# One statistic of LayerNorm moved behind a cast in VectorE's queue, in the first microseconds of an attention kernel

## The chip, the cores and the metric

The kernel runs on one core of one Trainium2 chip. The metric is the device time of one execution in microseconds (us), lower is better. Executions of one kernel are compared only in the undisturbed ("fast") state; all runs told here were in it, with a granted TensorE clock of 0.998 to 1.0. The "span" in a profile is the part of the execution that the profiler covers; in all runs here it is about 1.8 us shorter than the time.

Names: PE is TensorE's matmul side, PEld its weight loads, DVE is VectorE, ACT is ScalarE, POOL is GpSimd, SP is SyncE, whose queue issues many of the DMAs. "Landing" is the moment at which a DMA's data has arrived.

## The reference, cut to what matters

```python
xn = layernorm(A_x)                          # x: 2048 x 640
q  = (xn @ wq) -> 32 heads of 192
o  = softmax(q @ k_cache.T * 192**-0.5) @ v_cache   # per head, 2048 queries, 2048 keys
g  = silu( (silu(xn @ w1) * (xn @ w3)) @ w2 )
out = A_x + (o @ wo) * g
```

All is bfloat16. Attention over 32 heads is nearly the whole work.

## The kernel before

The kernel works through 32 heads, in each through four blocks `qb` of 512 queries, in each block through eight pairs `p` of key tiles. x is normalised in four blocks of 512 rows, `g` = 0 to 3, each of four tiles of rows. Block 0 and half of block 1 are normalised before the loop, the rest during head 0, between its matmuls. So during head 0 VectorE has two jobs: the LayerNorm of the next blocks, and the casts that take projected queries out of PSUM.

PSUM tiles with the tag `st2` share two buffers. Scores, projections and the transposes of x all take one of them in turn, so a late release of one of these tiles stops PE.

```python
def ln_stats(g, i):                      # VectorE: mean and variance of tile i of block g
    ...
    xr = x_sb[:, 4 * g + i, :].rearrange("p (a f) -> p a f", a=nsub)
    for a in range(nsub):
        nc.vector.bn_stats(out=stats[:, a, :], in_=xr[:, a, :])
    nc.vector.bn_aggr(out=mv[:, i, :], in_=stats[:])
    ...

def ln_turn(g, i2, copy):                # PE turns two normalised tiles; `copy` takes them from PSUM
    pst = ps_st.tile([P, 2, DC, P], BF16, tag="st2", name="pst")
    ...  # 10 transposes
    copy(out=xnT[...], in_=pst[:])

def swap_halves(g):                      # xnS is xnT with its partition halves exchanged, by DMA
    nc.sync.dma_start(out=xnS[0:64, :, qs], in_=xnT[64:P, :, qs])
    nc.sync.dma_start(out=xnS[64:P, :, qs], in_=xnT[0:64, :, qs])

def two_products(W, qs):                 # projection of a later head, in two row groups of 64
    ps = ps_st.tile([P, 1024], F32, tag="st2", name="ps")
    for j in range(2 * DC):
        for r in range(2):
            rows = slice(r * 64, (r + 1) * 64)
            xs = xnT if j % 2 == r else xnS
            nc.tensor.matmul(ps[:, r * 512:(r + 1) * 512], lhsT=W[rows, j, :], rhs=xs[rows, j // 2, qs],
                             start=(j == 0), stop=(j == 2 * DC - 1))
    return ps

def cast_pair(qAB, ps):                  # the two halves of ps, on two engines
    a = nc.vector.tensor_copy(out=qAB[0][:], in_=ps[:, 0:512])
    b = nc.scalar.copy(out=qAB[1][:], in_=ps[:, 512:1024])
    ...

# head_start(), before the loop; the order on SyncE's queue matters here
    ...
    swap_halves(0)
    ...
    load_v(0, (1,))        # second half of head 0's V, 384 KB, wanted at pair 4
    load_x(2)              # rows of block 2, 640 KB
    ...
    ln_turn_dma(1, 0); ln_turn_dma(1, 1)     # two tiles of block 1 turned by DMA
    for g in range(3, NQB):
        load_x(g)

def first_head(qb, p):                   # called at the end of each pair of head 0
    if qb == 0 and p == 1:
        ln_norm(1, 2, nc.vector)
        ln_norm(1, 3, nc.vector)
    if qb == 0 and p == 3:
        ln_turn(1, 1, nc.vector.tensor_copy)
        swap_halves(1)
    g = qb + 2
    if g < NQB:
        i = p - 2 if qb == 0 else p - 1
        if 0 <= i < 4:
            ln_stats(g, i)
        ...

for n, (h, qb, p) in enumerate(stream):
    ...
    if h == 0 and qb == 0 and p == 3:
        project(1, 0)                    # two_products, cast_pair, then moves of the result
    if h == 0 and qb + 1 < NQB and p == (5 if qb == 0 else 4):
        project0(qb + 1)                 # head 0's next queries, from xnT alone
    scores(n + 2)
    values(n)
    ...
    if h == 0:
        first_head(qb, p)
```

## Time and profile before

| | before |
|---|---|
| median of the first three runs | 1939.9 us (1939.57 to 1941.53) |
| the execution that was profiled | 1939.16 us, span 1937.4 us |
| PE busy in the span | 1927.5 us |
| PE's wait for the cast of head 1's first query | 0.75 us, once |

The page's first part gives busy time by engine, and its chain part says what the chain of work that ended last consists of:

```profile
span 1937.4 us, 59668 instructions
PE 1927.5 (99%) x27273; PEld 1316.9 (68%) x27281; DVE 654.4 (34%) x997; ACT 1180.1 (61%) x1278; POOL 282.4 (15%) x501
...
PE 98%; DMA 1%; DVE 1%; ACT 0%; SPq 0%; issue 0%; DVEq 0%; ACTq 0%
```

The chain is PE nearly throughout. Busy matmul time says little about how near PE is to its best, since pipelined matmuls look smaller in the trace (the Trainium skill, "Perfetto Trace Analysis", "Identifying the Most-Contended Engine", says so and asks for other measures; a_behind below has a loss of 0.42 us inside a stretch that counts as busy throughout). But the trace does show where PE stands still, and that is what this change is after. The list of PE's waits in the first 100 us (columns: who, on which line, for whom, total us, times, longest):

```profile
PE pk L569 <- POOL ident_bf masks.py:199: 2.8, 1, 2.8
PE pst L354 <- DVE qA L429: 0.8, 1, 0.8
PE st L487 <- ACT pT L490: 0.3, 1, 0.3
PE pst L354 <- DVE xn L346: 0.3, 1, 0.3
PE st L483 <- DVE qA L393: 0.2, 1, 0.2
```

The second line is the one. The timeline shows how it comes about. Its columns are start, duration, engine, line, operation, output and inputs, count; in brackets stands how long the engine was idle before and what ended that.

```profile
21.27 0.38 PE L424 MATMUL ps<-xnT,W 64*128 64x512 bf16 x1
...
21.69 0.58 ACT L430 CAST qB<-ps 128x512 bf16<-128x512 f32 x1 [1.74 <-PE ps L424]
...
21.97 0.89 DVE L316 BATCH_NORM_STATS2 stats<-x_all 128x6 f32<-128x320 bf16 x2 [0.60 <-DMA x_all<-in_A_x_dram]
22.12 0.84 PE L516 MATMUL obank<-vt,pT 64*128 64x193 bf16 x16
...
22.89 0.21 DVE L317 BATCH_NORM_AGGREGATE mv<-stats 128x2 f32<-128x12 f32 x1
23.02 0.64 DVE L429 CAST qA<-ps 128x512 bf16<-128x512 f32 x1
...
23.71 0.73 PE L354 MATMUL pst<-ident_bf,xn 128*128 128x128 bf16 x10 [0.75 <-DVE qA L429]
...
24.48 0.82 DVE L356 COPY xnT<-pst 128x1280 bf16<-128x1280 bf16 x1 [0.83 <-PE pst L354]
```

The projection (L424) is done at about 21.65 us. ScalarE casts its half at once. VectorE's cast is equally ready, but the statistics of block 2's first tile are ahead of it in VectorE's queue, and they wait until 21.97 us for the rows of block 2. PE ends its value products (L516) at 22.96 us and then needs the buffer for the transposes (L354), which can start only when the cast has ended, at 23.71 us.

### The profile page before, as it was taken

How to read it: one execution, taken by the hardware profiler on the slowest of the kernel's cores; microseconds unless marked ns; L12 is line 12 of the kernel's file. 1: busy time of each engine (PE TensorE's matmuls, PEld its weight loads, DVE VectorE, ACT ScalarE, POOL GpSimd, SP SyncE). 2: the span in 40 equal slices, each digit the busy share in tenths (PEclk: the TensorE clock that was granted, in tenths of full speed). 3: DMA queues.
4: the chain of work that ended last, by engine and by line, in shares of the span. 5: the costliest groups of instructions: out<-in, count | busy, mean ns of one | idle time of the engine just before them, and what ended most of it. 6: DMA issues, size and time to landing. Idle time of an engine off the chain costs nothing.

```text
span 1937.4 us, 59668 instructions
## 1 busy us (share of the span) xinstructions
PE 1927.5 (99%) x27273; PEld 1316.9 (68%) x27281; DVE 654.4 (34%) x997; ACT 1180.1 (61%) x1278; POOL 282.4 (15%) x501
## 2 busy tenths in 40 slices
PE   9999999999999999999999999999999999999998
PEld 6666666666666666666666666666666666577776
DVE  7333333333333333333333333333333334521111
ACT  6667676767676767776777777677767677210000
POOL 3111111111111111111111111111111110000000
PEclk9999999999999999999999999999999999999999
DMA  8643433323333434363434343434334220937872
GB/s 179 131 101 66 100 68 80 88 60 89 59 88 64 98 64 98 68 162 68 101 64 101 69 101 69 101 64 100 69 67 97 59 68 2 251 76 138 152 151 62
DMA packets 394643, 178.98 MB, mean 92 GB/s; under 512 B 341616, under 2 KB 382832, under 8 KB 394384
## 3 DMA queue, kind: packets, MB, share of 16 engines
q1 hardware_dynamic: 371136, 125.32, 31.5%
q0 software_dynamic: 19472, 45.71, 10.1%
q8 instruction: 215, 3.52, 0.8%
q10 hardware_dynamic: 3776, 4.06, 0.7%
q14 instruction: 44, 0.36, 0.1%
HBM read 52.82 MB, written 27.79 MB: 42 GB/s over the span
## 4 chain that ended last, share of the span: by engine, by line
PE 98%; DMA 1%; DVE 1%; ACT 0%; SPq 0%; issue 0%; DVEq 0%; ACTq 0%
PE obank L516 35%; PE st L487 33%; PE ps L424 14%; PE ps_s L111 11%; PE ps_f L727 3%; PE ps_gu L701 1%; DMA x_all<-in_A_x_dram 1%; PE st L488 1%; PE ps L410 0%; DVE stats L316 0%; ACT KW L277 0%; PE pst L354 0%; ACT xnT L356 0%; DVE qA L429 0%; SPq L289 0%
## 5 line engine op out<-in xcount | busy, mean ns | idle before, releaser
L490 ACT ACTIVATE pT<-st 128x1024 bf16<-128x1024 f32 x1024 | 1046.2, 1022 | 250.9 <-PE st L488 235.3
L516 PEld LDWEIGHTS <-pT 64*128 64x128 bf16 x16384 | 711.6, 94 | 241.9 <-ACT pT L490 0.2
L516 PE MATMUL obank<-vt,pT 64*128 64x193 bf16 x16384 | 849.6, 243 | 0.0
L487 PE MATMUL st<-qC,KW 64*128 64x512 bf16 x2046 | 605.8, 376 | 0.1
L525 DVE COPY osum<-obank 128x772 f32<-128x772 f32 x128 | 123.1, 962 | 787.1 <-PE obank L516 787.1
L488 PE MATMUL st<-qB,KW 64*128 64x512 bf16 x1024 | 385.2, 376 | 0.0
L487 PE MATMUL st<-qA,KW 64*128 64x512 bf16 x1022 | 384.5, 376 | 0.4 <-ACT pT L490 0.3
L488 PE MATMUL st<-qC,KW 64*128 64x512 bf16 x1022 | 384.5, 376 | 0.0
L488 PE MATMUL st<-qA,KW 64*128 64x512 bf16 x1022 | 384.4, 376 | 0.0
L487 PEld LDWEIGHTS <-KW 64*128 64x128 bf16 x3068 | 278.5, 94 | 153.7 <-issue 2.1
L424 PE MATMUL ps<-xnT,W 64*128 64x512 bf16 x1280 | 297.2, 376 | 0.0
L424 PE MATMUL ps<-xnS,W 64*128 64x512 bf16 x1280 | 296.3, 376 | 0.0
L488 PEld LDWEIGHTS <-KW 64*128 64x128 bf16 x3068 | 278.8, 94 | 0.7 <-issue 0.6
L377 POOL DMA_DIRECT2D qC<-qA x124 | 65.4, 527 | 1284.5 <-DVE rl_all L532 1268.3
L430 ACT CAST qB<-ps 128x512 bf16<-128x512 f32 x131 | 76.7, 585 | 228.2 <-PE ps L424 222.7
L111 PE MATMUL ps_s<-wo_sb,oT 128*128 128x384 bf16 (+3 forms) x1535 | 208.8, 299 | 0.1
L424 PEld LDWEIGHTS <-W 64*128 64x128 bf16 x2560 | 123.1, 94 | 121.1
L111 PEld LDWEIGHTS <-oT 128*128 128x128 bf16 x1536 | 148.3, 98 | 60.5
L526 DVE TENSOR_TENSOR osum<-osum,obank 128x772 f32<-128x772 f32 x128 | 122.7, 959 | 13.4
L533 DVE TENSOR_TENSOR ostage<-osum,rl_all 128x768 bf16<-128x768 f32 x128 | 122.6, 958 | 6.2 <-DMA o_scr<-ostage 1.9
L465 DVE SCALAR_TENSOR_TENSOR hT<-pt,qB 64x512 bf16<-64x512 bf16 x64 | 43.8, 684 | 197.4 <-ACT pt L464 197.4
L429 DVE CAST qA<-ps 128x512 bf16<-128x512 f32 x131 | 90.6, 691 | 25.0 <-PE ps L410 7.2
(84 smaller groups left out, 623.7 us busy)
## 6 DMA issues: line engine op xcount, KB each, us to landing
o_scr<-ostage SPq DMA_DIRECT2D x16, 1536.0 KB, 10.6
vt<-in_A_v_cache_dram SPq DMA_DIRECT2D x63, 384.0 KB, 6.0
qC<-qA POOLq DMA_DIRECT2D x248, 64.0 KB, 1.9
qC<-qB POOLq DMA_DIRECT2D x124, 64.0 KB, 2.4
wo_sb<-in_A_wo_dram POOLq DMA_DIRECT2D x1, 7680.0 KB, 37.3
W<-in_A_wq_dram POOLq DMA_DIRECT2D x32, 160.0 KB, 3.6
W<-in_B_w_dram POOLq DMA_DIRECT2D x32, 80.0 KB, 3.3
W<-in_A_wq_dram POOLq DMA_DIRECT2D x32, 80.0 KB, 2.9
```

The source lines that it names most:

```text
L111: nc.tensor.matmul(ps[:, 0:w], lhsT=oT[:, k, :], rhs=wo_sb[:, k, c0:c1], start=(k == 0), stop=(k == OC - 1))
L377: nc.gpsimd.dma_start(out=qC[0:64, half, :], in_=qAB[half][64:P, :])
L424: nc.tensor.matmul(ps[:, r * 512:(r + 1) * 512], lhsT=W[rows, j, :], rhs=xs[rows, j // 2, qs], start=(j == 0), stop=(j == 2 * DC - 1))
L429: a = nc.vector.tensor_copy(out=qAB[0][:], in_=ps[:, 0:512])
L430: b = nc.scalar.copy(out=qAB[1][:], in_=ps[:, 512:1024])
L487: nc.tensor.matmul(st2[:, 0:512], lhsT=ka, rhs=qa, start=r == 0 and nr == 3, stop=r == nr - 1)
L488: nc.tensor.matmul(st2[:, 512:1024], lhsT=kb, rhs=qb2, start=r == 0 and nr == 3, stop=r == nr - 1)
L490: nc.scalar.activation(out=pT2[:], in_=st2[:], func=ACT.Exp, scale=att_scale)
L516: nc.tensor.matmul(obanks[r][:, j * 256:j * 256 + DH + 1], lhsT=pT2[r * 64:(r + 1) * 64, t * 512 + j * P:t * 512 + (j + 1) * P], rhs=vt[r ...
L525: nc.vector.tensor_copy(out=osum[:], in_=ov[0])
L526: nc.vector.tensor_tensor(out=osum[:], in0=osum[:], in1=ov[1], op=ALU.add)
L533: nc.vector.tensor_tensor(out=ostage[:, qb * 4:qb * 4 + 4, hg * DH:(hg + 1) * DH], in0=osum[:, :, 0:DH], in1=rl.unsqueeze(2).to_broadcast( ...
```

## The change

The intent is to let the cast pass. The statistics of tile 0 of block 2 are no longer issued at the end of pair 2. They are issued at the end of pair 3, which is after the cast of the projection and before the copy of the transposes.

```diff
         if qb == 0 and p == 3:
+            ln_stats(2, 0)
             ln_turn(1, 1, nc.vector.tensor_copy)
             swap_halves(1)
         g = qb + 2
         if g < NQB:
             i = p - 2 if qb == 0 else p - 1
-            if 0 <= i < 4:
+            if 0 <= i < 4 and (qb, p) != (0, 2):
                 ln_stats(g, i)
```

No instruction is added or removed. On VectorE one cast goes ahead of two BN_STATS and one aggregation; no other engine's order changes.

## The prediction

> **What bounds the kernel now.** TensorE. The page gives PE 1927.5 us busy of a span of 1937.4, and the chain that ended last is 98% PE. From 80 us to the end of the attention (1750 us) PE is busy 1669.84 of 1670.00. So the only time to be had is in the few idle gaps of PE at the start. Quarter-microsecond stretches of the first 130 us show 4.67 us of PE idle: 2.77 before the first matmul, and after that only one large gap, 22.96 to 23.71 us. In the list of PE's waits it is "pst L354 <- DVE qA L429", 0.75 us (0.8 in the list), once.
>
> **How that gap comes about (timeline, 20 to 26 us).** In pair 3 of head 0's first block PE projects head 1's first query (L424, finished about 21.65). Its two halves lie in one PSUM buffer of two. ScalarE casts its half at once (21.69 to 22.27). VectorE's cast (0.64 us) stands in its queue behind the statistics of block 2's first rows, and these wait for the load of block 2's rows of x: VectorE idles 0.60 us until 21.97, then 0.89 us statistics, 0.21 aggregation. The cast runs 23.02 to 23.66. PE has ended the value products at 22.96, but its next transposes (L354) want the same PSUM buffer, so they start at 23.71. The Trainium skill, "PSUM — Partial Sum Buffer", section "Engine vs sequencer instructions", says that VectorE's queue is strict FIFO: a ready cast can't pass a waiting statistic. The trace agrees (cast ready at 21.69, started 23.02).
>
> **What the change does.** Nothing is added or removed. The order listing shows one difference on VectorE: the cast goes ahead of two BN_STATS and one aggregation. Other engines keep their order.
>
> Expected times, from those durations:
> - cast 21.7 to 22.35, before PE needs the buffer (22.96): the 0.75 us gap closes.
> - statistics from 22.35 (data landed 21.97) to about 23.45 with aggregation. The copy of the transposes (L356) gets its input 0.77 us after they start, about 23.72, so the statistics fit in front of it, with about 0.25 us to spare.
> - next scores need exp 5's PSUM buffer, whose exp ends at 23.41 as before; PE wants it at 23.63. Free.
> - copy 23.72 to 24.54, projection L410 about 25.05 instead of 25.80: the slack of 0.5 us stays.
> - query shifts (POOL) are issued 1.3 us earlier; no one waits for them.
>
> **How much stays.** Everything after hangs on PE, so all shifts by 0.75 us. Possible give-back: project(1,1) at 32.02 needs the swapped halves (second copy issued 26.01, 5.2 us to landing, so about 31.3); moved earlier they overlap more with the load of block 3 (issued 20.9, 5.4 us). Also L410 at 39.90 follows the DMA transposes' landing (39.75) by 0.15 us. Either may give back some tenths. I count 0.7 us.
>
> **Prediction.** 1939.9 - 0.7 = 1939.2 us, range 1938.3 to 1940.3. The spread of before (1939.57 to 1941.53) is larger than the gain, so the verdict is "same". Faster by over 2%: 0.005; within 2%: 0.99; slower: 0.005.
>
> **What the profile would show.** PE's wait "pst <- qA" gone (under 0.1 us), VectorE's 0.60 us wait for x_all gone or under 0.1, cast starting at about 21.7, transposes at about 22.96, L410 at about 25.05, PE idle after 20 us about 0.3 us instead of 1.05; total PE busy unchanged.
>
> **What would make it wrong.** x's block 2 landing over 1 us later, so that the copy of the transposes, not the cast, holds PE; a new wait at L424 (32 us) or L410 (40 us) for DMAs that do not come earlier; or run-to-run spread of a microsecond, which would hide the gain or reverse its sign.

## The result, and the profile after

| | before | after |
|---|---|---|
| median, six runs each | 1939.86 us | 1938.49 us |
| range | 1939.19 to 1941.53 | 1938.43 to 1939.14 |
| span of the profiled execution | 1937.4 us | 1936.7 us |
| PE idle from 20 to 130 us, in quarter-microsecond stretches | 1.04 us | 0.16 us |

(The 0.16 us are three gaps of 0.05 us, each in a group of ten L410 products of which the trace shows nine. So they may be missing records and not idle time; before has three such gaps too.)

The ratio of after to before is 0.9992 with a 95% interval of 0.9979 to 1.0005. A ratio is the mean time of one kernel's fast runs over that of the other's of the same rounds, so it is not quite the ratio of the medians in the table.

The page and the list of PE's waits of the changed kernel:

```profile
span 1936.7 us, 59668 instructions
PE 1927.1 (100%) x27273; PEld 1317.2 (68%) x27281; DVE 654.4 (34%) x997; ACT 1181.5 (61%) x1278; POOL 282.1 (15%) x501
...
PE 99%; DVE 0%; DMA 0%; ACT 0%; issue 0%
```

```profile
PE pk L569 <- POOL ident_bf masks.py:199: 2.8, 1, 2.8
PE pst L354 <- DVE xn L346: 0.8, 1, 0.8
PE st L487 <- ACT pT L490: 0.3, 1, 0.3
PE st L483 <- DVE qA L393: 0.2, 1, 0.2
```

The wait for `qA` at L429 is gone. (The wait for `xn` lies at 7 to 8 us, before the two kernels differ. The warm-up matmuls before it leave PE idle for longer or shorter; the transposes start at 7.8 and 7.9 us all the same.) The timeline, as before:

```profile
21.77 0.59 ACT L430 CAST qB<-ps 128x512 bf16<-128x512 f32 x1 [1.74 <-PE ps L424]
21.77 0.69 DVE L429 CAST qA<-ps 128x512 bf16<-128x512 f32 x1 [0.31 <-PE ps L424]
...
22.20 0.85 PE L516 MATMUL obank<-vt,pT 64*128 64x193 bf16 x16
22.38 0.88 DVE L316 BATCH_NORM_STATS2 stats<-x_all 128x6 f32<-128x320 bf16 x2
...
22.98 0.73 PE L354 MATMUL pst<-ident_bf,xn 128*128 128x128 bf16 x10
23.29 0.21 DVE L317 BATCH_NORM_AGGREGATE mv<-stats 128x2 f32<-128x12 f32 x1
...
23.75 0.82 DVE L356 COPY xnT<-pst 128x1280 bf16<-128x1280 bf16 x1 [0.25 <-PE pst L354]
```

Both casts start together at 21.77 us. The transposes follow the value products without a gap. VectorE still idles 0.25 us before the copy, so the statistics fit between the two. The transposes come 0.73 us earlier than before (22.98 against 23.71), and the span is 0.7 us shorter: nothing of it was given back in this execution.

The medians, however, differ by 1.37 us, twice the gap that the profile shows, and the changed kernel's runs lie closer together: five of six within 0.18 us. That was not predicted, and the experiments are about it.

### The profile page after: what moved, and what is told of

It reads as the page before. It is cut to its first block, busy times and chain, and to the rows that moved or that the text cites. A ratio compares the mean times of both kernels' runs of the same rounds, so it can differ in the third digit from the quotient of the medians.

```text
span 1936.7 us, 59668 instructions
## 1 busy us (share of the span) xinstructions
PE 1927.1 (100%) x27273; PEld 1317.2 (68%) x27281; DVE 654.4 (34%) x997; ACT 1181.5 (61%) x1278; POOL 282.1 (15%) x501
## 4 chain that ended last, share of the span: by engine, by line
PE 99%; DVE 0%; DMA 0%; ACT 0%; issue 0%
PE obank L516 35%; PE st L487 34%; PE ps L424 14%; PE ps_s L111 11%; PE ps_f L728 3%; PE ps_gu L702 1%; PE st L488 1%; PE ps L410 0%; DMA x_all<-in_A_x_dram 0%; DVE stats L316 0%; PE ps L391 0%; PE pst L354 0%; PE pk L271 0%; ACT pT L490 0%; DVE mv L317 0%
## 5 line engine op out<-in xcount | busy, mean ns | idle before, releaser
L488 PE MATMUL st<-qB,KW 64*128 64x512 bf16 x1024 | 385.0, 376 | 0.0
L488 PE MATMUL st<-qC,KW 64*128 64x512 bf16 x1022 | 384.3, 376 | 0.0
L488 PE MATMUL st<-qA,KW 64*128 64x512 bf16 x1022 | 384.3, 376 | 0.0
L424 PE MATMUL ps<-xnT,W 64*128 64x512 bf16 x1280 | 297.3, 376 | 0.0
L424 PE MATMUL ps<-xnS,W 64*128 64x512 bf16 x1280 | 296.2, 376 | 0.0
L488 PEld LDWEIGHTS <-KW 64*128 64x128 bf16 x3068 | 278.5, 94 | 0.8 <-issue 0.6
L424 PEld LDWEIGHTS <-W 64*128 64x128 bf16 x2560 | 123.6, 94 | 120.7
L429 DVE CAST qA<-ps 128x512 bf16<-128x512 f32 x131 | 90.6, 692 | 25.3 <-PE ps L410 7.2
```

The costliest lines, as they stand in the source:

```text
L488: nc.tensor.matmul(st2[:, 512:1024], lhsT=kb, rhs=qb2, start=r == 0 and nr == 3, stop=r == nr - 1)
```

## The experiments

Four calls, each on another chip, each with runs of the kernel before beside it. Every run below is "same" as the kernel before (each 95% interval of the ratio contains 1), so what follows rests on medians, spreads and traces. Names that start with `b_` are made from the kernel before, with `a_` from the changed one. The expectations name these theories.

- Theory L: PE's wait is for the load. The kernel before pays, microsecond for microsecond, for the landing of block 2's rows, which varies from run to run. The changed kernel has slack there.
- Rival N: the spread is noise that both kernels share, and the true gain is 0.75 us.
- Rival Q: not the load, but the place in the queue costs the time.
- Theory S and rival T came later: the slow runs that the changed kernel still has come from the swapped halves of block 0 landing late (S), or from elsewhere (T).

### The changed kernel again: a_again and a_third

No edit.

> The changed kernel once more, unchanged. Theory L (the kernel before pays, microsecond for microsecond, for when block 2's rows of x land, and that moment varies from run to run; the changed kernel has slack there): the changed kernel's runs lie within about 0.3 us of each other near 1938.5, those of the kernel before spread over 1 to 2 us above 1939.2, so the mean gain (1.2 to 1.6 us) is larger than the 0.75 us gap of the profiled run. Rival N (the spread is noise of the chip or of the first loads at the start, which both kernels share): the changed kernel spreads as widely as the one before, and with more runs the gain settles at 0.75 us.

> The changed kernel a third time, as the yardstick on the chip of this call. From eleven runs so far: most within 1938.3 to 1938.7, one in five or six about 0.6 us slower. No theory tells this run apart; it gives the others their reference.

Measured: 1938.61 us median (1938.34 to 1939.21) against 1939.47 (1938.5 to 1940.54, nine runs of before); then 1938.44 (1938.32 to 1938.82) against 1939.28 (1938.87 to 1940.06). In each case the changed kernel's spread is smaller, and the medians differ by 0.86 and 0.84 us. The expected mean gain of 1.2 to 1.6 us did not come: the means differ by 0.90 and 0.95 us.

### The order of before, with data that is there: b_nodata

```diff
             if 0 <= i < 4:
-                ln_stats(g, i)
+                ln_stats(g, i, 4 if (qb, p) == (0, 2) else None)   # read a row tile of block 1 instead
```

`ln_stats` takes the tile to read as a third argument. The result is wrong on purpose; every instruction stands where it stood and takes as long.

> The kernel before, order of instructions the same, but the first statistic of block 2 reads rows of block 1, which landed long ago (wrong result on purpose, same length). Theory L: VectorE's 0.60 us wait for x goes; the cast starts about 22.4 and ends about 23.05, so PE still waits about 0.1 to 0.2 us of the 0.75 for the cast behind 1.1 us of statistics; times about 0.6 us above the profile-equal of the changed kernel minus that, so 1938.6 to 1938.9, and with a spread as small as the changed kernel's. Rival Q (it is the place in the queue, not the load, that costs): PE still waits 0.5 us or more. Rival N: spread as in the kernel before.

Measured: 1938.57 us median, and all five runs between 1938.53 and 1938.63. The timeline:

```profile
21.29 0.88 DVE L316 BATCH_NORM_STATS2 stats<-x_all 128x6 f32<-128x320 bf16 x2
...
22.34 0.64 DVE L429 CAST qA<-ps 128x512 bf16<-128x512 f32 x1
...
23.03 0.73 PE L354 MATMUL pst<-ident_bf,xn 128*128 128x128 bf16 x10
```

The statistics stand ahead of the cast as before, yet PE idles only 0.06 us (in the quarter-microsecond stretches). So the place in the queue costs next to nothing when the data is there, and rival Q falls. With the load gone from the cast's path, the spread of the five runs is 0.10 us, against 2.04 us for the nine runs of before. Rival N does not fit that.

### The load issued earlier: b_early and a_early

```diff
-        load_v(0, (1,))
-        load_x(2)
+        load_x(2)
+        load_v(0, (1,))
```

> The kernel before with block 2's rows of x issued ahead of head 0's second half of V on the same queue, right result. Theory L: the rows land 1 us or more earlier than 21.97, the wait of 0.60 us goes and PE waits 0.1 to 0.2 us for the cast: 1938.6 to 1938.9 us, small spread, so most of the change's gain without moving any instruction of VectorE. V's second half is wanted only at about 25 us, so nothing waits for it. Rival Q: PE's wait stays at 0.5 us or more.

> Both: the changed order, and the earlier issue of block 2's rows. Theory L: PE has no wait left here already, so the same as the changed kernel within 0.1 us (1938.4 to 1938.6); if the changed kernel's odd slow run (1939.14 of six) comes from this load, it goes. If the earlier load helped something else, it would be faster by more than 0.2 us.

Measured, with the right result: b_early 1938.56 us median (1938.37 to 1938.93); a_early 1939.45 (1938.43 to 1939.81). The trace of b_early:

```profile
21.16 0.88 DVE L316 BATCH_NORM_STATS2 stats<-x_all 128x6 f32<-128x320 bf16 x2
...
22.20 0.64 DVE L429 CAST qA<-ps 128x512 bf16<-128x512 f32 x1
...
22.89 0.73 PE L354 MATMUL pst<-ident_bf,xn 128*128 128x128 bf16 x10
```

The statistics start at 21.16 us without waiting, the cast at 22.20, and PE idles 0.06 us. So the earlier load alone, with VectorE's order untouched, wins as much as the change (a_again: 1938.61), as theory L has it.

Both together are worse than either in three of five runs (1939.45, 1939.78, 1939.81), which no theory expected. The profiled execution of a_early was one of its two fast ones (1938.43 us) and shows no new wait, so its trace does not tell why.

### The load made later: b_late and a_late

```diff
         load_v(0, (1,))
+        load_x(3, 0, 2)         # half of block 3 ahead of block 2
         load_x(2)
...
-        for g in range(3, NQB):
-            load_x(g)
+        load_x(3, 2, 4)
```

> The kernel before with half of block 3's rows of x (320 KB) issued ahead of block 2's on the same queue, so block 2 lands 1 to 2 us later; right result. Theory L: the delay goes into the time one for one, since the cast stands behind the wait: PE's wait for the cast grows from 0.75 us by the delay of the landing, 1941 to 1942 us. Rival N: no change beyond the spread.

> The changed kernel with the same later load. Theory L: the cast is not touched (starts at about 21.8), transposes on time; the statistics now delay the copy of the transposes behind them, which has about 0.25 us in hand and then 0.5 us until the projection wants it. So the loss is the landing's delay beyond 21.97 less about 1.1 to 1.2 us: 0 to 0.9 us, against 1 to 2 us in the kernel before. Rival N: as the changed kernel.

Measured: b_late 1941.46 us median (1940.09 to 1942.42, four runs), a_late 1939.46 (1939.14 to 1940.61, four runs), before 1939.80 (1939.36 to 1940.16, seven runs). The trace of b_late:

```profile
23.14 0.89 DVE L316 BATCH_NORM_STATS2 stats<-x_all 128x6 f32<-128x320 bf16 x2 [1.85 <-DMA x_all<-in_A_x_dram]
...
24.19 0.64 DVE L429 CAST qA<-ps 128x512 bf16<-128x512 f32 x1
...
24.88 0.73 PE L354 MATMUL pst<-ident_bf,xn 128*128 128x128 bf16 x10 [2.00 <-DVE qA L429]
```

The landing came 1.17 us later than in the first trace of before (23.14 against 21.97), PE's wait grew by 1.25 us to 2.00, and the span by 1.3 us to 1938.7. That is the one-for-one payment. (The two runs of 1942.33 and 1942.42 us were not traced; how much of their time is this wait stays open.) Now a_late:

```profile
21.23 0.39 PE L424 MATMUL ps<-xnS,W 64*128 64x512 bf16 x2 [1.61 <-DMA xnS<-xnT]
...
24.80 0.73 PE L354 MATMUL pst<-ident_bf,xn 128*128 128x128 bf16 x10
24.96 0.89 DVE L316 BATCH_NORM_STATS2 stats<-x_all 128x6 f32<-128x320 bf16 x2 [0.68 <-DMA x_all<-in_A_x_dram]
...
26.01 0.77 DVE L356 COPY xnT<-pst 128x1280 bf16<-128x1280 bf16 x1
26.12 0.83 PE L516 MATMUL obank<-vt,pT 64*128 64x193 bf16 x16
...
26.88 1.47 PE L410 MATMUL ps<-xnT,W 128*128 128x512 bf16 x6
...
29.65 0.68 DVE L429 CAST qA<-ps 128x512 bf16<-128x512 f32 x1
...
31.46 0.84 PE L516 MATMUL obank<-vt,pT 64*128 64x193 bf16 x16
```

And the same stage of the changed kernel, from its first trace, in which L410 starts at 25.06 us:

```profile
27.44 0.68 DVE L429 CAST qA<-ps 128x512 bf16<-128x512 f32 x1
...
28.65 0.38 PE L487 MATMUL st<-qA,KW 64*128 64x512 bf16 x1
...
29.30 0.83 PE L516 MATMUL obank<-vt,pT 64*128 64x193 bf16 x16
```

Two things are to be seen. First, the slack. The statistics start 0.16 us after the transposes here. In the first trace of before they started 0.99 us ahead of the moment at which PE was ready for the transposes (21.97 against 22.96), and cost 0.75 us. So, counted from where PE stands, the rows landed 1.15 us later (0.16 + 0.99), and up to L410 PE lost nothing: the copy ends at 26.78 us, and the projection L410, which needs it, follows the value products at once. But VectorE is now behind. Its next cast starts 2.77 us after L410, where the changed kernel has 2.38, and the value products behind the scores that use this cast (31.46 us) start 4.58 us after L410, where the changed kernel has 4.24 (29.30). So the late rows cost 0.34 us, none of it as a gap of PE (a_behind below shows how such a loss hides). The expected slack of 1.1 to 1.2 us looked only as far as L410; it was too large. Still, the kernel before, paying one for one, would have lost about 1.9 us (an estimate: its 0.75 and the 1.15), and with the later load the medians of the two kernels differ by 2.0 us.

Second, a new wait that I had not foreseen: PE stood 1.61 us at L424 for the swapped halves of block 0. With the uneven start of the two row groups it cost 1.96 us (from the first product at 19.25 us to the transposes 5.55 us pass, in the changed kernel 3.59). The two losses, less 0.17 us that comes back at the next projection, make up the 2.1 us by which this span exceeds the changed kernel's. The two swaps took 9.0 us (median) from issue to landing, where those in the first trace of before took 6.7 us and those in b_late, which has the same loads, 7.1 us; a_late is the only one of the traces in which PE waits for them. The profiled run was a_late's slowest, 1940.61 us; the other three, without a trace, are 1939.14 to 1939.52.

### The statistics one place further back: a_behind

```diff
         if qb == 0 and p == 3:
-            ln_stats(2, 0)
             ln_turn(1, 1, nc.vector.tensor_copy)
+            ln_stats(2, 0)
```

> The changed kernel with the statistics of block 2's first rows one place further back, behind the copy of the transposes. The copy has 0.25 us of idle VectorE in front of it in the changed kernel, and the statistics take 1.1 us, so everything behind comes 0.8 to 0.9 us later on VectorE: the next cast (27.44 us) would start at about 28.3, and the scores that take its PSUM buffer at 28.65 would wait about 0.4 us. Expected: 0.3 to 0.6 us slower than the changed kernel, still faster than before. If VectorE has more slack than that, the same as the changed kernel.

Measured: 1939.31 us median, all four runs between 1939.17 and 1939.34, span 1937.4 us. That is 0.7 us more than the changed kernel's span, a little more than expected, and as much as the first pair of profiles showed as the gain. Against the runs of before (median 1939.80) it is still 0.49 us faster, so the gain is not all lost. The timeline shows where:

```profile
28.35 0.68 DVE L429 CAST qA<-ps 128x512 bf16<-128x512 f32 x1
...
29.07 0.29 DVE L413 COPY qC<-qA 64x512 bf16<-64x512 bf16 x1
29.09 0.39 PE L487 MATMUL st<-qA,KW 64*128 64x512 bf16 x1 [0.27 <-DVE qA L429]
...
29.41 0.37 PE L488 MATMUL st<-qC,KW 64*128 64x512 bf16 x1
...
30.16 0.84 PE L516 MATMUL obank<-vt,pT 64*128 64x193 bf16 x16
```

VectorE is behind by 0.9 us, and the next cast starts at 28.35 us where the changed kernel has 27.44. PE shows 0.27 us of idle for it. The rest is hidden: the six score matmuls before the value products take 1.07 us (29.09 to 30.16) where the changed kernel takes 0.65 (28.65 to 29.30), because they need VectorE's late copies to `qC` (the first ends at 29.36 us, and L488, which reads it, starts at 29.41). PE counts as busy while either of its two row groups works: 1.07 of 1.07 us here. The value products start 0.86 us later than in the changed kernel (30.16 against 29.30); 0.17 us of this is back at 36.39 us (against 35.70), after a projection at which the changed kernel itself loses 0.13 us. That leaves the 0.7. That the four runs lie so close together would fit a load still further from PE's path, but only one of them was traced.

### What makes the changed kernel's slow runs: a_early_noswap, a_order, a_early_order

Of the first eleven runs of the changed kernel two took about 0.6 us more than the rest. a_late's wait suggested the swap of block 0 (theory S). Three kernels take it out of PE's path. In a_early_noswap, which has the earlier load as well, head 1's first projection reads `xnT` where it should read `xnS` (wrong):

```diff
-                xs = xnT if j % 2 == r else xnS
+                xs = xnT if j % 2 == r or not swapped else xnS      # swapped is False for head 1, block 0
```

In a_order and a_early_order the five products that need no swap come first, in both row groups (right result); the latter has the earlier load as well. The `start` and `stop` flags go by `s`, which the cut leaves out:

```diff
-        for j in range(2 * DC):
-            for r in range(2):
+        for s in range(2 * DC):
+            for r in range(2):
+                j = 2 * (s % DC) + (r if s < DC else 1 - r)
```

> The changed kernel with the earlier load of block 2, and head 1's first projection reads the unswapped x in place of the swapped (wrong result on purpose, the same matmuls). Theory S: the slow runs that are left (three of five with the early load, two of eleven with the change alone) come from the swapped halves of block 0 landing later than PE wants them at about 19.4 us[...]. Then all five runs lie within 0.2 us of 1938.5. Rival T: they come from elsewhere (the first loads, V, the later swaps or transposes); then about three of five stay 0.8 to 1.3 us slower, as with the early load alone.

> The changed kernel, and the two-row-group projection takes the five products that read unswapped x first and the five that read swapped x last, in both row groups; right result. Under theory S this gives the swap about 1.1 us more to land, at no cost in matmuls: median as the changed kernel (1938.4 to 1938.6), no run over 1938.8, and no late start of xnS matmuls at 31 us. Under rival T the same number of slow runs as the changed kernel. If the order of the products costs PE anything, it shows as more time in all 128 projections.

> The same reordered projection with the early load of block 2; right result. The early load gave slow runs in three of five. Theory S: the slow runs shrink from about 1.2 us to 0.1 us or vanish: all within 1938.3 to 1938.7. Rival T: about three of five stay at 1939.4 to 1939.8.

Measured, beside a_third's median of 1938.44: a_early_noswap 1938.68 (1938.4 to 1939.3), a_order 1938.58 (1938.39 to 1939.39), a_early_order 1938.79 (1938.54 to 1939.33). Each has a run of about 1939.3 us, which theory S had excluded. So S, as the sole cause, falls. Rival T's "three of five stay 0.8 to 1.3 us slower" is not met either. a_early itself was not run on this chip, so how much the two edits helped it stays open.

The trace of a_early_order, of its second slowest run (span 1937.1 us), holds another small wait, at the projection of head 0's next queries, for the tiles of block 1 that are turned by DMA:

```profile
PE ps L410 <- DMA xnT<-xn: 0.2, 1, 0.2
```

It explains 0.2 of the 0.5 us by which this span exceeds a_order's. So what is left seems to be several DMAs of the start with little slack, of which the traces caught three, once each: the swap (a_late), block 2's rows themselves (a_late) and these turned tiles. No slow run of the changed kernel itself was traced. This is not settled. None of these versions beats the changed kernel.

### A second trace of the kernel before: b_again

No edit. It tests theory L on one execution whose landing nobody chose.

> The kernel before, once more, for a second trace of it and more of its times. Theory L ties three readings of one execution to each other, whatever the load does in it: PE's wait W for the cast is the landing of block 2's rows less about 21.2 us (the first trace: landing 21.95, wait 0.75), and the span is about 1936.6 to 1936.7 us plus W, within 0.2 us. So a span of 1937.8 goes with a wait of 1.1 to 1.2 us and a landing at about 22.3. Rival N: the span moves and the wait stays at 0.75 us.

Measured: 1939.25 us median (1938.86 to 1939.53). The profiled execution took 1939.53 us with a span of 1937.8 us:

```profile
22.26 0.89 DVE L316 BATCH_NORM_STATS2 stats<-x_all 128x6 f32<-128x320 bf16 x2 [0.97 <-DMA x_all<-in_A_x_dram]
...
23.30 0.64 DVE L429 CAST qA<-ps 128x512 bf16<-128x512 f32 x1
...
24.00 0.73 PE L354 MATMUL pst<-ident_bf,xn 128*128 128x128 bf16 x10 [1.12 <-DVE qA L429]
```

A landing at about 22.2 us, a wait of 1.12 us and a span of 1937.8 us are nearly the example that the expectation gave (22.3 us, 1.1 to 1.2, 1937.8). Six traces line up (a_late, a_behind and a_early_order have other losses besides):

| trace | statistics start | PE's wait for the cast | span |
|---|---|---|---|
| after | (not ahead of the cast) | 0 | 1936.7 |
| b_early | 21.16 | 0.06 | 1936.7 |
| b_nodata | 21.29 | 0.06 | 1936.8 |
| before | 21.97 | 0.75 | 1937.4 |
| b_again | 22.26 | 1.12 | 1937.8 |
| b_late | 23.14 | 2.00 | 1938.7 |

Span less wait is 1936.6 to 1936.7 in all six. The two further traces of the changed kernel have spans of 1936.7 and 1936.8 us (a_third, a_again). Rival N, a wait that stays at 0.75 us whatever the span, is out.

### All runs of the two kernels together

Counting every run of the kernel before (45) and of the changed kernel (16), the means are 1939.64 and 1938.59 us, with standard deviations of 0.61 and 0.26 us. The gain is 1.05 us (standard error 0.11, worked out from these deviations), half of a tenth of a per cent. The fastest run of before, 1938.50, is as fast as the changed kernel's median over these runs: an execution in which, on theory L, the rows came early enough. The traces with the load in its old place have it landing between 21.6 and 22.2 us, so they show waits of up to 1.12 us. The two slowest runs of before, 1941.53 and 1941.61, were not traced; that they too wait for this load is not shown.

## Why the prediction was right or wrong

The predicted 1939.2 us and its range of 1938.3 to 1940.3 hold the measured 1938.49 us. That owes something to the width of the range: the gain came out at twice the count and still lies inside.

- The mechanism was right in each step. The cast starts at 21.77 us (predicted 21.7), the transposes at 22.98 (22.96), the copy at 23.75 (23.72), with 0.25 us in hand (0.25), and L410 at 25.06 (25.05). The wait for the cast and VectorE's wait for x are gone.
- FIFO order, for which the prediction quoted the Trainium skill ("PSUM — Partial Sum Buffer", "Engine vs sequencer instructions"), is what the trace shows: a cast ready at about 21.7 us started at 23.02 us behind a waiting statistic, and at 21.77 us once it stood ahead.
- The possible give-back at the next projection (predicted at "project(1,1)") came, and cost nothing. In the changed kernel the first product that needs the swapped halves starts 0.13 us after its neighbour (31.41 against 31.28 us), since the second swap, issued 0.36 us earlier, takes 5.7 us to land instead of 5.2. The kernel before had a wait of about as much a little later, at 35.65 us, for a late cast, which the changed kernel no longer has. The tally is even. At 39 us PE did not wait, as hoped.
- The size was off: "I count 0.7 us". The term that was mis-sized is the wait of 0.75 us, read from one execution and taken for the kernel's. It is one draw of something that varies: 0.75 us in the first trace, 1.12 in the second, and about 1.05 on average, if the pooled mean gain is taken for it. A sign of it stood in the record beforehand: the profiled execution took 1939.16 us, 0.4 us less than the fastest of the first three timed runs. Adding its distance to the six-run median (0.70 us) to the wait gives 1.45 us, near the recorded 1.37.
- The prediction named "x's block 2 landing over 1 us later" as a risk to the gain, looking at the changed kernel alone. Against the kernel before it is the reverse: that one pays all of a later landing (1.25 us more wait in b_late), while the changed one lost 0.34 us by a landing 1.15 us later (a_late). So a later landing of this size makes the gain larger.

Not settled: what makes one changed run in eight 0.6 us slower (2 of 16 were above 1939), and why the earlier load and the change together gave more slow runs than either alone.

## What to carry to other kernels

In an in-order queue, put the work that frees a PSUM buffer ahead of work that waits for a DMA, if the latter has slack behind it; but look at what stands behind that place too, for one step further back cost 0.7 us (a_behind). When a wait hangs on a DMA's landing, its length in one profile is a sample: compare the time of the profiled execution with the median before taking the wait as the gain. A fix of the load (b_early) and a fix of the order (the change) can each be enough, and the two together need not be better.

## What the Trainium skill lacked or had wrong

- "DMA: Bandwidth & Descriptors" gives no figure for how far the landing of one and the same DMA moves from run to run. Here the same 640 KB load on the same queue took 8.3 us from issue to landing in one execution of the kernel before and 8.7 us in another, and the swaps of 320 KB took 7.1 and 9.0 us (medians of two) in b_late and a_late, which issue the same loads; the 45 runs of before lie between 1938.50 and 1941.61 us, five with the load taken out of the path within 0.10 us.
- The same page, "Issuing engines are not separate DMA queues", calls the issue time "usually small relative to the DMA itself". For this load the issue took SyncE 1.56 of the 8.3 us in the first trace of before, and 0.91 of 7.6 us in the changed kernel's. That is no contradiction, but here it is more than the slack of 0.25 us.
- "Perfetto Trace Analysis", "Optimization Strategy", says to find the gaps of the bottleneck engine and what ends them. That worked for 0.75 us here. It lacks that gaps can be invisible where PE runs two row groups: in a_behind the listed gap was 0.27 us and the loss 0.7 us, and the late rows of a_late cost 0.34 us with no gap listed at all.
